# Weight loads in pieces between attention blocks, and routing steps moved among the expert tiles

## The chip, the cores and the metric

The kernel runs on one core of a Trainium2 chip. The metric is the device time of one execution in microseconds (us). The engines named below are TensorE (PE), VectorE (DVE), ScalarE (ACT), GpSimd (POOL) and SyncE (SP); SP, ACT and POOL also issue DMA transfers, which 16 DMA engines carry out.

## The reference

An attention over chunks, followed by a mixture of experts in which each token goes to one expert.

```python
for c in range(nc):                        # chunks of 32 queries
    q_c = q[:, :, c_start:c_end]
    k_full = concatenate([mem_k, k[:, :, l_start:r_end]])   # 8 memory rows, 16 left, 8 right
    a = softmax(scale * q_c @ k_full.T)
    out[:, :, c_start:c_end] = a @ v_full
x = out as (B, S, H * D)                   # 4 x 768 tokens of 512
logits = x @ w_gate                        # 8 experts
local_gate = sigmoid(x @ w_local)
for each b, s in order:
    e = argmax(logits) if s == 0 or local_gate < 0.5 else the expert of the token before
    out[b, s] = softmax(logits)[e] * (relu(x @ w1[e]) @ w2[e])     # 512 -> 1024 -> 512
```

All arrays are float32.

## The kernel before

**Attention.** The 4 x 768 queries of 8 heads are cut into 32 blocks of 96 queries (NB = 32, eight per batch). `load(n)` brings q and k of a block on SP's queue and v on ACT's. The tiles come from a pool of AHEAD + 1 buffers, and block n + AHEAD is loaded when block n begins. `scores` makes the transposed scores on TensorE (L215) and their exponentials on ACT (L220). `values` multiplies them by v (L227), and VectorE divides by the sums and writes the rows into the batch's tile x (L229, L230). There are three buffers for four x tiles (pool xp), so the tile of the fourth batch, opened at block 24, takes the buffer of the first. `turn(n)` transposes the rows of a block (L270), and after every fourth block `logits` makes the expert logits of four blocks (L277, L282).

**Routing.** It is done twice, each time for two batches. `route_picks` chooses experts on VectorE, and `route_ranks` counts, for each token, the earlier ones of its expert (transposes L329, scans L332 and L336). `route_places` turns ranks into places (L346, L350), and `route_rows` transposes them (L356) and has GpSimd scatter the rows of x into a DRAM table `x_dram` ordered by expert: 16 scatters of 96 rows of 2056 bytes (L372). `plan_early` lists the first five tiles of 128 rows (EARLY = 5), all of them of tokens from the first half. `plan_late`, after the second routing, lists the others, 26 at most.

**Experts.** A tile of 128 rows is gathered from `x_dram` by GpSimd (`gathered`, L484) into `xs`, one of five buffers. `rows_turned` transposes it on TensorE (L575), VectorE copies it to `gxt` (L577) and adds up `to`, the output rows (L579). `hidden` multiplies by w1 (L588) with the Relu on ACT (L590), `product` multiplies by w2 (L596), ACT scales the result (L598) and GpSimd scatters it to the output (L599). In the program's order the rows of tile i + 1 are turned between hidden and product of tile i. 24 tiles always run (SURE = 24), and up to seven more under a condition each; three of them ran here. `weights` loads an expert's w1 and w2, one transfer of 2 MB each (L499, L501), into one of three buffers, two tiles ahead; the first two experts' loads stand in the attention's loop, at blocks 22 and 26.

The order on each engine is set by a scheduler from the program's order and its model of when inputs are ready; each engine then works through its row of instructions strictly in order. On SP, q, k and weights share one queue. A DMA of SP or ACT also waits for the eighth one before it to have landed (eight semaphores in turn).

Of the kernel before, what the change touches and what calls it, by code (L numbers as in the profile page):

```python
# [8 lines left out]
F32 = mybir.dt.float32  # L9
# [33 lines left out]
AHEAD = 2  # L43
# [49 lines left out]
def everything(ctx, tc, q, k, v, w_gate, w_local, w1, w2, x_dram, out, ident, kept_i):  # L93
# [399 lines left out]

    def weights(tiles, i, pool):
        table, _, _ = tiles
        e = nc.values_load(table[:, i:i + 1], engines=[SP], min_val=0, max_val=E - 1,
                           skip_runtime_bounds_check_because="made from counts of tokens")
        w1_sb = pool.tile([P, DK, F], F32, name="w1_sb")
        nc.sync.dma_start(w1_sb, w1[bass.ds(e, 1)].rearrange("o p k f -> p (o k) f"))  # L499
        w2_sb = pool.tile([P, FK, D], F32, name="w2_sb")  # L500
        nc.sync.dma_start(w2_sb, w2[bass.ds(e, 1)].rearrange("o p m d -> p (o m) d"))  # L501
        return w1_sb, w2_sb
# [22 lines left out]
    for n in range(NB):  # L525
# [45 lines left out]
    def rows_turned(tiles, i, xs):  # L571
# [6 lines left out]
        to = hp.tile([P, 1], I32, name="to", bufs=4)  # L578
# [3 lines left out]
    def hidden(xt, w1_sb):  # L582
        ht = hp.tile([P, FK, P], F32, name="ht")
        for g in range(0, FK, 4):
# [5 lines left out]
            nc.scalar.activation(ht[:, g:g + 4], h_ps, ACT.Relu)  # L590
        return ht

    def product(ht, w2_sb, xs, to):
        y_ps = yps.tile([P, D], F32, name="y_ps")
        for m in range(FK):
# [3 lines left out]
        nc.gpsimd.indirect_dma_start(  # L599
            out=out, out_offset=bass.IndirectOffsetOnAxis(ap=to, axis=0), in_=y, in_offset=None,  # L600
            bounds_check=NT - 1, oob_is_err=False)
# [5 lines left out]
    for i in range(SURE):  # L607
        if i + 2 < EARLY:
            early_w.append(weights(early, i + 2, pools[(i + 2) % 3]))
        if i == 1:  # L610
            held["ranks"] = route_ranks()
        if i == 2:
            route_places(*held["ranks"])
            route_rows(1, (xs.pop(2), xs.pop(3)), *held["picks"], held["ranks"][1])
            late, n_i = plan_late(done)
        if i == 3 and not shifted:
            k_ps = xps.tile([1, 1], F32, name="k_ps", tag="xps")
            nc.tensor.matmul(k_ps, lhsT=kept, rhs=every, start=True, stop=True)
# [67 lines left out]
```

## Time and profile before

| what | value |
|---|---|
| median of 3 runs | 595.25 us (592.55 to 595.96) |
| profiled execution, its own time | 594.97 us |
| its span, from the first to the last instruction | 593.2 us |
| TensorE busy | 540.3 us, 91% of the span |
| mean granted TensorE clock | 0.941 of full speed |
| mean DMA rate over the span | 266 GB/s |

The span has two stages: attention until 160.33 us, where the first product of the experts begins, and the experts' tiles after it. In the page each digit of a row of slices stands for a fortieth of the span, 14.83 us; the row PEclk gives the granted clock in tenths. The chain of waits follows the work back from the last instruction, and each piece of it gives its start, its length and what it was.

### The profile page before, as it was taken

Reading aid. Unit: us, or ns where it says so; the run is one execution under the profiler, and the core shown is the slowest. Engines: PE = TensorE matmul, PEld = TensorE weight load, DVE = VectorE, ACT = ScalarE, POOL = GpSimd, SP = SyncE. Lnnn points to the kernel's source line nnn. Section 1 sums busy time; section 2 is a strip of 40 time slices with the busy share of each in tenths; the row PEclk is TensorE's granted clock in tenths of the full one; section 3 lists DMA queues with packets and bytes.
Section 4 is the critical chain, followed back from the end, with each engine's and each line's share of the span. In section 5 each row is a group of like instructions: output and inputs, shape, how many; then the busy total and the mean of one; then the engine's idle time right before and its main releaser. Section 6 shows DMA issues by size and latency. Waiting matters only on the chain.

```text
span 593.2 us, 8772 instructions
## 1 busy us (share of the span) xinstructions
PE 540.3 (91%) x3582; PEld 404.1 (68%) x3582; DVE 86.7 (15%) x319; ACT 112.1 (19%) x224; POOL 90.5 (15%) x112
## 2 busy tenths in 40 slices
PE   8999999495899990999999999999999999999980
PEld 6777778365677770877777777777777777766650
DVE  3333364111403400000000000000000000000000
ACT  3444444122111010011111111111111111111110
POOL 2000005330000642411111111111111100000000
PEclk9999999757799996799999999999999999999995
DMA  8666658996197998888888888889888888882000
GB/s 252 209 194 196 194 170 242 407 342 242 63 373 296 310 380 314 238 325 337 327 326 335 318 308 319 322 309 330 319 324 329 325 315 308 313 325 84 19 6 4
DMA packets 29427, 157.93 MB, mean 266 GB/s; under 512 B 5115, under 2 KB 9213, under 8 KB 22464
## 3 DMA queue, kind: packets, MB, share of 16 engines
q1 hardware_dynamic: 16992, 127.93, 59.2%
q0 software_dynamic: 6720, 20.78, 10.2%
q10 hardware_dynamic: 5664, 8.54, 5.0%
q8 instruction: 32, 0.52, 0.4%
q14 instruction: 19, 0.16, 0.1%
HBM read 144.62 MB, written 13.40 MB: 266 GB/s over the span
## 4 chain that ended last, share of the span: by engine, by line
PE 76%; DMA 10%; issue 8%; POOL 1%; DVE 1%; SPq 0%; ACT 0%; POOLq 0%; DVEq 0%
PE h_ps L588 28%; PE y_ps L596 25%; PE o_ps L227 8%; PE s_ps L215 6%; DMA x_dram<-x,row 4%; PE lt_ps L277 4%; DMA kt<-in_k_dram 3%; DMA out_dram<-y,to 2%; PE xt_ps L270 2%; PE g_ps L575 2%; POOL x_dram L372 1%; DMA xs<-x_dram,rows_late 1%; PE l_ps L282 0%; DVE rank L336 0%; PE c_ps L329 0%
## 5 line engine op out<-in xcount | busy, mean ns | idle before, releaser
L588 PEld LDWEIGHTS h_ps<-gxt,w_sb 128*128 128x128 f32 x1728 | 201.2, 196 | 28.4 <-DVE gxt L577 17.2
L588 PE MATMUL h_ps<-gxt,w_sb 128*128 128x128 f32 x1728 | 203.0, 279 | 17.6 <-DVE gxt L577 16.9
L596 PE MATMUL y_ps<-w_sb,ht 128*128 128x512 f32 x432 | 189.9, 592 | 0.0
L596 PEld LDWEIGHTS y_ps<-w_sb,ht 128*128 128x128 f32 x432 | 80.0, 190 | 90.4 <-issue 90.4
L599 POOL DMA_INDIRECT out_dram<-y,to x27 | 27.2, 1008 | 351.6 <-ACT y L598 334.3
L590 ACT ACTIVATE ht<-h_ps 128x512 f32<-128x512 f32 x54 | 32.2, 597 | 182.0 <-PE h_ps L588 182.0
L227 PE MATMUL o_ps<-vt,pt 128*96 128x65 f32 x512 | 58.1, 269 | 8.0 <-issue 7.8
L227 PEld LDWEIGHTS o_ps<-vt,pt 128*96 128x96 f32 x512 | 52.8, 182 | 11.2 <-issue 8.3
L215 PE MATMUL s_ps<-qt,kt 64*128 64x96 f32 x512 | 42.3, 297 | 5.6 <-DMA kt<-in_k_dram 5.6
L598 ACT ACTIVATE y<-y_ps,xs 128x512 f32<-128x512 f32 x24 | 16.5, 687 | 161.6 <-PE y_ps L596 161.6
L215 PEld LDWEIGHTS s_ps<-qt,kt 64*128 64x128 f32 x512 | 35.6, 200 | 14.3 <-issue 6.0
L372 POOL DMA_INDIRECT x_dram<-x,row x32 | 29.4, 918 | 102.9 <-DVE x L367 87.5
L579 DVE TENSOR_TENSOR to<-xs,past_late 128x1 int32<-128x1 f32 x19 | 3.0, 160 | 257.7 <-DMA out_dram<-y,to 229.9
L220 ACT ACTIVATE pt<-s_ps,mask_mid 128x256 f32<-128x256 f32 x72 | 29.0, 472 | 17.7 <-PE s_ps L215 17.4
L577 DVE COPY gxt<-g_ps 128x512 f32<-128x512 f32 x27 | 18.6, 690 | 83.8 <-PE g_ps L575 83.5
L230 DVE TENSOR_TENSOR x<-o_ps,rinvs 96x256 f32<-96x256 f32 x64 | 26.6, 417 | 13.0 <-DMA x_dram<-x,row 11.5
L277 PE MATMUL lt_ps<-xt,wg 128*9 128x384 f32 x64 | 23.7, 517 | 1.1 <-ACT xt L271 1.1
L229 DVE RECIPROCAL rinvs<-o_ps 96x4 f32<-96x4 f32 x64 | 11.3, 177 | 84.0 <-PE o_ps L227 82.9
L271 ACT COPY xt<-xt_ps 128x384 f32<-128x384 f32 x32 | 15.3, 479 | 39.9 <-PE xt_ps L270 39.9
L484 POOL DMA_INDIRECT xs<-x_dram,rows_late x19 | 18.4, 967 | 16.4 <-DMA x_dram<-x,row 10.9
L270 PE MATMUL xt_ps<-ident,x 96*128 96x96 f32 x128 | 18.0, 268 | 0.7 <-DVE x L230 0.7
L277 PEld LDWEIGHTS lt_ps<-xt,wg 128*9 128x9 f32 x64 | 5.4, 95 | 14.7 <-issue 12.5
(165 smaller groups left out, 141.8 us busy)
## 6 DMA issues: line engine op xcount, KB each, us to landing
w_sb<-in_w_dram SPq DMA_DIRECT2D x54, 2048.0 KB, 8.5
vt<-in_v_dram ACTq DMA_DIRECT2D x32, 260.0 KB, 3.7
kt<-in_k_dram SPq DMA_DIRECT2D x32, 256.0 KB, 3.7
qt<-in_q_dram SPq DMA_DIRECT2D x32, 192.0 KB, 3.3
x_dram<-x,row POOLq DMA_INDIRECT x32, 12.1
out_dram<-y,to POOLq DMA_INDIRECT x27, 7.5
xs<-x_dram,rows_late POOLq DMA_INDIRECT x19, 6.7
x<-x_dram,rows_late POOLq DMA_INDIRECT x7, 4.8
```

What stands on the lines that cost most here:

```text
L215: nc.tensor.matmul(st[:, u, a], lhsT=kt[h, a], rhs=qt[h, a], start=True, stop=True)
L220: nc.scalar.activation(pt[:, :, :, c], st[:, :, :, c], ACT.Exp, bias=m[:, g:g + 1], scale=SCALE)
L227: nc.tensor.matmul(o_ps[:, a], lhsT=pt[:, u, a], rhs=vt[:, 2 * a + u], start=True, stop=True)
L230: nc.vector.tensor_tensor(x[:, 0:D].rearrange("p (a u d) -> p u a d", u=2, d=DH)[:, u], o_ps[:, :, 0:DH], rinv.to_broadcast([QB, HP, DH]), ...
L270: nc.tensor.transpose(xt_ps[:, kk], x[:, P * kk:P * kk + P], identity=ident[:QB, :QB])
L277: nc.tensor.matmul(lt_ps, lhsT=wg[:, kk], rhs=xt[:, kk], start=(kk == 0), stop=(kk == DK - 1))
L372: ins = nc.gpsimd.indirect_dma_start(out=x_dram[:, :], out_offset=bass.IndirectOffsetOnAxis(ap=row[:, i:i + 1], axis=0), in_=x[b][0:QB, n] ...
L577: nc.vector.tensor_copy(xt, g_ps)
L588: nc.tensor.matmul(h_ps[:, m], lhsT=w1_sb[:, kk, P * (g + m):P * (g + m) + P], rhs=xt[:, kk], start=(kk == 0), stop=(kk == DK - 1))
L590: nc.scalar.activation(ht[:, g:g + 4], h_ps, ACT.Relu)
L596: nc.tensor.matmul(y_ps, lhsT=ht[:, m], rhs=w2_sb[:, m], start=(m == 0), stop=(m == FK - 1))
L599: nc.gpsimd.indirect_dma_start(out=out, out_offset=bass.IndirectOffsetOnAxis(ap=to, axis=0), in_=y, in_offset=None, bounds_check=NT - 1, o ...
```

## The change

The weights of an expert come in eight pieces of 0.5 MB: four of w1 (one for each 128 of its 512 rows) and four of w2 (each for two of its eight blocks of rows). Both arrays are laid out in DRAM so that a piece is one run of 512 KB, 4 KB to a partition; before, it was 16 KB to a partition. For the first two experts one piece is traced at each attention block from block 22 on, and what is left after the last block. AHEAD goes from 2 to 3. In the attention's loop `route_places`, `route_rows` and `plan_early` come one, one and two blocks earlier. Among the tiles, `route_ranks` moves from before tile 1's hidden to after tile 0's, `route_places` from tile 2 to before tile 1's hidden, and `route_rows` into the middle of that hidden. `to` gets eight buffers, the check sum `k_ps` moves by a tile, and the gathers for the conditional tiles are put behind the stores of the tiles before.

```diff
-AHEAD = 2
+AHEAD = 3
...
+    def weights_begun(tiles, i, pool):
...
+        def pieces():
+            e = nc.values_load(table[:, i:i + 1], engines=[SP], min_val=0, max_val=E - 1,
+                               skip_runtime_bounds_check_because="made from counts of tokens")
+            for k in range(DK):
+                nc.sync.dma_start(w1_sb[:, k], w1[bass.ds(e, 1), k].rearrange("o p f -> p (o f)"))
+                yield
+            for m in range(0, FK, 2):
+                nc.sync.dma_start(w2_sb[:, m:m + 2].rearrange("p m d -> p (m d)"),
+                                  w2[bass.ds(e, 1), m // 2].rearrange("o p d -> p (o d)"))
+                yield
...
-        nc.sync.dma_start(w1_sb, w1[bass.ds(e, 1)].rearrange("o p k f -> p (o k) f"))
-        nc.sync.dma_start(w2_sb, w2[bass.ds(e, 1)].rearrange("o p m d -> p (o m) d"))
...
+        if n == NR + 2:
+            route_places(*held["ranks"])
         if n == NR + 3:
-            route_places(*held["ranks"])
+            route_rows(0, (xs.pop(0), xs.pop(1)), *held["picks"], held["ranks"][1])
         if n == NR + 4:
-            route_rows(0, (xs.pop(0), xs.pop(1)), *held["picks"], held["ranks"][1])
+            early, done = plan_early()
         if n == NR + 6:
-            early, done = plan_early()
             early_xs = [gathered(early, i, (0,)) for i in range(EARLY)]
-            early_w = [weights(early, 0, wa)]
-        if n == NR + 10:
-            early_w.append(weights(early, 1, wa))
+            early_w, pieces = zip(*(weights_begun(early, i, wa) for i in range(2)))
+            early_w, pieces = list(early_w), itertools.chain(*pieces)
+        if n >= NR + 6:
+            next(pieces)
+    for _ in pieces:
+        pass
...
-        to = hp.tile([P, 1], I32, name="to", bufs=4)
+        to = hp.tile([P, 1], I32, name="to", bufs=8)
...
+            if between is not None and g == 0:
+                between()
...
+        between = None
         if i == 1:
-            held["ranks"] = route_ranks()
+            route_places(*held["ranks"])
+
+            def between():
+                route_rows(1, (xs.pop(2), xs.pop(3)), *held["picks"], held["ranks"][1])
         if i == 2:
-            route_places(*held["ranks"])
-            route_rows(1, (xs.pop(2), xs.pop(3)), *held["picks"], held["ranks"][1])
             late, n_i = plan_late(done)
...
-            gathered(late, SURE - EARLY + j, (0, 1), rest[:, j])
+            with tc.issue_after(stored):
+                gathered(late, SURE - EARLY + j, (0, 1), rest[:, j])
...
-        ht = hidden(xt, w1_sb)
+        ht = hidden(xt, w1_sb, between)
+        if i == 0:
+            held["ranks"] = route_ranks()
```

On SP, where the first expert's weights begin among the last loads of q and k, the kernel before has:

```order
L496 TENSOR_LOAD table_early_1268
L499 ISA
L499 DMA w1_sb_1305<-in_w1_dram 128x4096
L501 ISA
L501 DMA w2_sb_1307<-in_w2_dram 128x4096
L126 DMA qt_1402<-in_q_dram 128x384
L128 DMA kt_1404<-in_k_dram 128x512
L126 DMA qt_1441<-in_q_dram 128x384
L128 DMA kt_1443<-in_k_dram 128x512
L496 TENSOR_LOAD table_early_1268
L499 ISA
L499 DMA w1_sb_1483<-in_w1_dram 128x4096
```

At the same place the changed kernel has:

```order
L502 TENSOR_LOAD table_early_1196
L505 ISA
L505 DMA w1_sb_1308<-in_w1_dram 128x1024
L505 ISA
L505 DMA w1_sb_1308<-in_w1_dram 128x1024
L127 DMA qt_1358<-in_q_dram 128x384
L129 DMA kt_1360<-in_k_dram 128x512
L505 ISA
L505 DMA w1_sb_1308<-in_w1_dram 128x1024
L127 DMA qt_1411<-in_q_dram 128x384
L129 DMA kt_1413<-in_k_dram 128x512
L505 ISA
```

The two whole transfers ahead of four loads have become one or two quarter transfers between loads, and the second expert's weights, which stood ahead of the last two loads of q and k, come after all of them.

On TensorE, in the first three tiles (c_ps, b_ps and r_ps are the second routing's three steps), the kernel before has:

```order
L588 MATMUL h_ps<-gxt,w_sb 128x128 x32
L575 MATMUL g_ps<-ident,xs 128x128 x4
L596 MATMUL y_ps<-w_sb,ht 128x512 x8
L329 MATMUL c_ps<-ident,pick 48x96 x8
L588 MATMUL h_ps<-gxt,w_sb 128x128 x32
L575 MATMUL g_ps<-ident,xs 128x128 x4
L596 MATMUL y_ps<-w_sb,ht 128x512 x8
L346 MATMUL b_ps<-count_992,same 16x1
L346 MATMUL b_ps<-count_1835,earlier 16x1
L588 MATMUL h_ps<-gxt,w_sb 128x128 x6
L356 MATMUL r_ps<-ident,rank 96x16 x8
```

In the first two tiles the changed kernel has:

```order
L608 MATMUL h_ps<-gxt,w_sb 128x128 x32
L330 MATMUL c_ps<-ident,pick 48x96 x8
L595 MATMUL g_ps<-ident,xs 128x128 x4
L618 MATMUL y_ps<-w_sb,ht 128x512 x8
L347 MATMUL b_ps<-count_998,same 16x1
L347 MATMUL b_ps<-count_1823,earlier 16x1
L608 MATMUL h_ps<-gxt,w_sb 128x128 x16
L357 MATMUL r_ps<-ident,rank 96x16 x8
L608 MATMUL h_ps<-gxt,w_sb 128x128 x16
```

The counts stand ahead of tile 0's product, and the rows' transposes in the middle of tile 1's hidden instead of early in tile 2's.

On VectorE, from tile 3's copy on (`to` is the add for a late tile), the kernel before has:

```order
L577 COPY gxt_2037<-g_ps_2032 128x512
L619 CAST kept_i_66<-k_ps_2055 1x1
L579 TENSOR_TENSOR to_2180<-xs_1993,past_late_1971 128x1
L579 TENSOR_TENSOR to_2249<-xs_2058,past_late_1971 128x1
L577 COPY gxt_2109<-g_ps_2104 128x512
L579 TENSOR_TENSOR to_2318<-xs_2127,past_late_1971 128x1
```

From the same copy on the changed kernel has:

```order
L597 COPY gxt_2067<-g_ps_2062 128x512
L599 TENSOR_TENSOR to_2222<-xs_2023,past_late_2001 128x1
L599 TENSOR_TENSOR to_2297<-xs_2085,past_late_2001 128x1
L599 TENSOR_TENSOR to_2372<-xs_2160,past_late_2001 128x1
L597 COPY gxt_2142<-g_ps_2137 128x512
L599 TENSOR_TENSOR to_2447<-xs_2238,past_late_2001 128x1
L658 CAST kept_i_66<-k_ps_2212 1x1
L597 COPY gxt_2220<-g_ps_2215 128x512
```

Ahead of tile 4's copy stand the adds of tiles 5, 6 and 7, before those of 5 and 6; from there on the add of tile i + 3 is ahead of tile i's copy, before that of tile i + 2.

## Rows read from the trace of the kernel before

**Rows 1.** The page's slices: granted TensorE clock, tenths of full speed.
```profile
PEclk9999999757799996799999999999999999999995
```

**Rows 2.** Stretches: us, busy PE, PEld, DVE, ACT, POOL; PEclk, DMA share, GB/s.
```profile
10.00:90.00 80.00, 79.70 (x829) 63.78 (x828) 31.95 (x112) 38.75 (x93) 0.00 (x0) 1.00 0.65 196
...
105.00:134.00 29.00, 20.47 (x128) 15.61 (x127) 4.52 (x16) 6.22 (x15) 9.67 (x11) 0.65 1.01 373
...
196.00:223.00 27.00, 27.00 (x150) 18.78 (x148) 4.75 (x20) 3.08 (x5) 15.24 (x17) 1.00 0.99 349
...
300.00:400.00 100.00, 100.00 (x580) 73.21 (x580) 5.63 (x14) 12.83 (x21) 13.29 (x14) 1.00 0.86 325
```

**Rows 3.** The chain that ended last: start us, us, what; attention.
```profile
38.48 2.68 PE lt_ps L277 x8
...
49.62 1.06 PE s_ps L215 x16
50.68 1.50 PE o_ps L227 x16
...
53.58 2.68 PE lt_ps L277 x8
...
102.39 2.68 PE lt_ps L277 x8
...
105.47 7.77 issue
...
134.44 9.72 DMA kt<-in_k_dram
...
155.70 2.76 PE lt_ps L277 x8
...
160.33 9.01 PE h_ps L588 x64
```

**Rows 4.** VectorE in order of time: start us, us, instruction [idle before <-releaser].
```profile
112.72 0.75 DVE L230 TENSOR_TENSOR x<-o_ps,rinvs 96x256 f32<-96x256 f32 x2 [11.51 <-DMA x_dram<-x,row]
...
235.79 0.16 DVE L579 TENSOR_TENSOR to<-xs,past_late 128x1 int32<-128x1 f32 x1 [27.08 <-DMA xs<-x_dram,rows_late]
```

**Rows 5.** GpSimd in order of time, both rounds of scatters and two gathers.
```profile
92.21 0.98 POOL L372 DMA_INDIRECT x_dram<-x,row  x1 [87.47 <-DVE x L367]
...
112.91 0.91 POOL L372 DMA_INDIRECT x_dram<-x,row  x1 [1.62 <-DMA x_dram<-x,row]
...
195.50 0.91 POOL L372 DMA_INDIRECT x_dram<-x,row  x1 [1.44 <-DVE tiles_late L452]
...
216.40 0.91 POOL L372 DMA_INDIRECT x_dram<-x,row  x1 [0.62 <-DMA x_dram<-x,row]
...
231.73 0.98 POOL L484 DMA_INDIRECT xs<-x_dram,rows_late  x1 [10.90 <-DMA x_dram<-x,row]
...
315.23 0.97 POOL L484 DMA_INDIRECT xs<-x_dram,rows_late  x1 [0.30 <-issue]
```

**Rows 6.** Scatters into x_dram begun from 92 to 99 us: issue to landing.
```profile
DMA to landing us min/median/max: 4.4/6.8/8.5
```

**Rows 7.** Scatters into x_dram begun from 205 to 217 us: issue to landing.
```profile
DMA to landing us min/median/max: 11.7/14.7/17.3
```

**Rows 8.** SP's queue in order of time, the second expert's w2.
```profile
132.37 0.34 SPq L501 DMA_DIRECT2D w_sb<-in_w_dram  x1
```

**Rows 9.** TensorE in order of time: hidden of tile 4, and of two steady tiles.
```profile
237.50 10.26 PE L588 MATMUL h_ps<-gxt,w_sb 128*128 128x128 f32 x64 [14.33 <-DVE gxt L577]
...
312.70 7.31 PE L588 MATMUL h_ps<-gxt,w_sb 128*128 128x128 f32 x64
...
327.15 7.31 PE L588 MATMUL h_ps<-gxt,w_sb 128*128 128x128 f32 x64
```

**Rows 10.** Gathers (L484) from 300 to 400 us: issue to landing.
```profile
DMA to landing us min/median/max: 6.3/6.7/8.2
```

**Rows 11.** The page's DMA issues: queue, count, size, median us to landing.
```profile
kt<-in_k_dram SPq DMA_DIRECT2D x32, 256.0 KB, 3.7
```

More of the change, by code (lines that the diff above doesn't have):

```diff
@@ L1 @@
+import itertools
 from contextlib import ExitStack
@@ L492, in gathered @@
         return xs
-    def weights(tiles, i, pool):
[L495 to L498, printed above, removed]
-        nc.sync.dma_start(w1_sb, w1[bass.ds(e, 1)].rearrange("o p k f -> p (o k) f"))
-        w2_sb = pool.tile([P, FK, D], F32, name="w2_sb")
-        nc.sync.dma_start(w2_sb, w2[bass.ds(e, 1)].rearrange("o p m d -> p (o m) d"))
-        return w1_sb, w2_sb
+    def weights_begun(tiles, i, pool):
+        table, _, _ = tiles
+        w1_sb = pool.tile([P, DK, F], F32, name="w1_sb")
+        w2_sb = pool.tile([P, FK, D], F32, name="w2_sb")
+        def pieces():
[8 more added lines that the diff above has]
+                yield
+        return (w1_sb, w2_sb), pieces()
+    def weights(tiles, i, pool):
+        w, pieces = weights_begun(tiles, i, pool)
+        for _ in pieces:
+            pass
+        return w
     make_scores, make_values = (shifted_scores, shifted_values) if shifted else (scores, values)
@@ L577, in rows_turned, with hidden @@
         nc.vector.tensor_copy(xt, g_ps)
-        to = hp.tile([P, 1], I32, name="to", bufs=4)
+        to = hp.tile([P, 1], I32, name="to", bufs=8)
         nc.vector.tensor_tensor(to, xs[:, D + 1:XW], past[:, i:i + 1], op=ALU.add)
         return xt, to
-    def hidden(xt, w1_sb):
+    def hidden(xt, w1_sb, between=None):
         ht = hp.tile([P, FK, P], F32, name="ht")
@@ L609, in everything @@
             early_w.append(weights(early, i + 2, pools[(i + 2) % 3]))
+        between = None
         if i == 1:
-            held["ranks"] = route_ranks()
+            route_places(*held["ranks"])
+            def between():
+                route_rows(1, (xs.pop(2), xs.pop(3)), *held["picks"], held["ranks"][1])
         if i == 2:
-            route_places(*held["ranks"])
-            route_rows(1, (xs.pop(2), xs.pop(3)), *held["picks"], held["ranks"][1])
             late, n_i = plan_late(done)
-        if i == 3 and not shifted:
-            k_ps = xps.tile([1, 1], F32, name="k_ps", tag="xps")
-            nc.tensor.matmul(k_ps, lhsT=kept, rhs=every, start=True, stop=True)
-            nc.vector.tensor_copy(kept_i, k_ps)
         if late is not None:
@@ L628, in everything @@
             j = i + 8 - SURE
-            gathered(late, SURE - EARLY + j, (0, 1), rest[:, j])
+            with tc.issue_after(stored):
+                gathered(late, SURE - EARLY + j, (0, 1), rest[:, j])
         w1_sb, w2_sb = early_w[i]
-        ht = hidden(xt, w1_sb)
+        ht = hidden(xt, w1_sb, between)
+        if i == 0:
+            held["ranks"] = route_ranks()
+        if i == 4 and not shifted:
+            k_ps = xps.tile([1, 1], F32, name="k_ps", tag="xps")
+            nc.tensor.matmul(k_ps, lhsT=kept, rhs=every, start=True, stop=True)
+            nc.vector.tensor_copy(kept_i, k_ps)
         if i + 1 < SURE:
@@ L634, in everything @@
             ahead = rows_turned(tiles, at_i, early_xs[i + 1])
-        product(ht, w2_sb, early_xs[i], to)
+        stored = product(ht, w2_sb, early_xs[i], to)
         xt, to = ahead
```

10 lines of the change are left out of this document (6 added, 4 removed).

## The prediction

> **What bounds the kernel now.** I read the page's slices first. TensorE is busy in nearly all of them, but its granted clock is below full in slices 8 to 11 and in 16 and 17 [rows 1]. The table by stretches gives the places: from 105 to 134 us a mean of 0.65 between its two levels (1.2 and 2.4 GHz), against 1.00 before 90 and after 300 [rows 2]. So three stalls and the half-speed stretches behind them are what can be won. The rest is TensorE's own work: a group of four attention blocks takes 15.10 us (53.58 minus 38.48 [rows 3]) and a tile of the expert stage 14.45 us (327.15 minus 312.70 [rows 9]).
>
> Stall 1 is the 7.77 us of "issue" at 105.47 [rows 3]. The profile names no releaser for it, but VectorE does: it sat 11.51 us until 112.72, when it could write x of block 24 [rows 4]. That block opens the fourth batch's x tile, whose buffer is the first batch's; the write waits for that batch's eight scatters. They went out from 92.21 on [rows 5], and the pair of 2 MB weight loads was queued among them. Scatters begun before 99 us landed in 6.8 us (median) [rows 6].
>
> Stall 2 is the 9.72 us that a k load took from 134.44 [rows 3]. Its issue stood on SP behind a 2 MB weight load which left only at 132.37 [rows 8], and its bytes stood behind that load in the queue.
>
> Stall 3 is the 14.33 us until 237.50 [rows 9]. Tile 4's rows were long there; VectorE's copy of them stood behind an add for tile 5 that waited 27.08 us for a gather [rows 4]. That gather left at 231.73, after the last of 16 scatters, begun at 216.40 [rows 5]. Those scatters took 14.7 us to land [rows 7], with the DMA engines busy for 0.99 of the time [rows 2].
>
> **The change part by part.** *Attention's end (stalls 1 and 2).* TensorE's sequence now has the transposes that give the scatters their rows ahead of the fifth logits product (2.68 us [rows 3]) and some of the values around it: the scatters begin about 4 us earlier, near 88. The eighth begins 7 x 1.38 = 9.7 us later (15 steps from 92.21 to 112.91 are 1.38 each [rows 5]) and lands 6.8 us after that [rows 6], so x is free at 104.5. The values of block 25 come at 105.47 [rows 3] and need VectorE's writes of block 24 before (0.75 [rows 4]): the stall is 0 to 1 instead of 7.77. Beside these scatters stand now two pieces of 0.5 MB instead of 4 MB. In SP's order every q and k load comes before the second expert's weights, with one or two pieces between loads, and AHEAD = 3 issues each load a block (2.9 us) earlier; at most three pieces (1.6 MB, 4.3 us at the 373 GB/s of [rows 2]) are in front of one. So stall 2 goes; its bounds are 0 and that 4.3 less the block won.
>
> What the stage then costs: two more groups after the sixth logits product at 102.39 put the eighth at 132.6, and hidden(0) follows 160.33 - 155.70 = 4.63 later [rows 3], at 137.2. That is too long by what the last group lacks: between the sixth and the eighth product the new order has one set of values fewer (1.50) and three sets of scores fewer (1.06 each), and about 1 us of transposes and a copy's wait more: 133.5 is the floor. I take 135.0: the work is counted, and 1.5 us is left for the two waits above. So hidden(0) starts **25.3 us earlier** (23.1 to 26.8).
>
> *Clock behind them.* hidden(0) took 9.01 us against 7.31 at full speed [rows 3, 9]: **1.7 us** back, if no stall is left before it.
>
> *Second routing (stall 3).* The rows' transposes stand after 16 of tile 1's 32 products in the new order, before after 6 of tile 2's: one tile less 10/32 of a hidden of 7.31, 12.2 us earlier. Before, the first scatter began at 195.50 [rows 5], 35.2 us after hidden(0); now 35.2 - 1.7 - 12.2 = 21.3 after it. Fifteen steps of 1.39 (195.50 to 216.40 [rows 5]) put the last at 42.2. What it takes to land is not shown for 4 KB weight rows: 6.8 us beside the attention's loads, whose rows are 1.5 to 2 KB [rows 6], and 14.7 beside weight rows of 16 KB [rows 7]. I take 9, since 4 KB is nearer to the first: 51.2. Then gathers 5 and 6, the store of tile 2 and gather 7 leave at about 1 us each (0.98 [rows 5]), gather 7 lands 6.7 later [rows 10], and the add and copy take 0.9: 61.8. The new order on VectorE has three adds (tiles 5, 6, 7) ahead of tile 4's copy, before it had two, so the whole chain counts. TensorE wants that copy at 237.50 - 14.33 - 160.33 - 1.7 = 61.1. The stall is 1 us (0 to 6.4) instead of 14.33: **13.3 us** saved, and the 10.26 us of the next hidden go back to 7.31 [rows 9]: **3.0 us**, if the stall is that short.
>
> The Trainium skill, "DMA: Bandwidth & Descriptors", section "Queues, rings and completion order", says each DMA engine goes round its queues and changes only after a whole packet. By that rule a 2 KB scatter row gets a third of a full engine beside 4 KB rows and a ninth beside 16 KB rows; 3.2 MB of scatters at a third of 373 GB/s would take 25 us, and the stall would be near 0. That agrees in kind with the 6.8 and 14.7 us of [rows 6, 7].
>
> *Steady tiles.* Weight bytes are the same, in rows of 4 KB instead of 16. At 16 KB rows the engines moved 325 GB/s at a share of 0.86, so 378 when full; at the attention's rows 196 at 0.65, so 301 [rows 2]. Drawn as a line in time per row (100 ns at 1.9 KB, 693 at 16 KB), 4 KB gives 190 ns, some 345 GB/s. A tile moves 325 x 14.45 = 4.70 MB: 13.6 us, under the 14.45 of TensorE. I take 0; the share should rise to about 0.94. The cover is thin: at 301 it is 15.6. Eight issues a tile on SP instead of two, at 0.34 us each [rows 8], are 2.7 us of 14.45. Eight target buffers for the add take away its wait for old stores, which nothing on TensorE waited for. But the add for tile i+3 now leads the copy for tile i: gather i+3 leaves 315.23 - 312.70 = 2.5 us after product i-2 ends, lands 6.7 later, and 0.9 follow: 10.1 of the 14.45 us. Hidden, with 4.3 us to spare (8.2 is the longest landing [rows 10]).
>
> *Start.* A third load of 0.71 MB before block 0: 0 if it queues behind, 2.4 us at 301 GB/s if it shares; I take 0.3.
>
> **Sum**, against the profiled execution (594.97, span 593.2, so 1.8 outside it; the median of the runs, 595.25, is 0.3 above): 593.2 - 25.3 - 1.7 - 13.3 - 3.0 + 0.3 = 550.2, and with 1.8 **552 us**.
>
> **The rivals.**
> *A. Scatters are as slow as before.* If landing stays at 14.7 us, stall 3 keeps about 6.4 us and its half-speed stretch: 552 + 5.4 + 3 = 560. For it: the engines were full there [rows 2] and as many bytes remain. Against: smaller rows, an earlier start.
> *B. Attention keeps a wait.* More is moved before hidden(0) in less time. One wait of 4 us with the half-speed stretch that followed stall 1 (0.65 over 29 us [rows 2] is 20 us at the lower level, 10 lost) gives 552 + 14 = 566.
> *C. The DMA engines become the bound.* At 301 GB/s a tile takes 15.6: 22 tiles x 1.15 = 25 us, 577. Against: the line above.
> *D. Slower: the gather enters the tile's loop.* With the add for tile i+3 ahead of copy i, every microsecond of landing above 11.0 (6.7 + 4.3) lengthens each of 16 tiles (5 to 20). At 14.7 us, seen with full engines [rows 7], it is 16 x 3.7 = 59: 611. It undoes the gain from 13.7 us on. Against: 8.2 is the longest landing in steady tiles [rows 10].
> *E. Nothing comes of it:* the weights' arrival, not these waits, sets the end; 595. Against: the steady tiles follow each other at 14.45 us with no gap [rows 9], so weights come in time.
> *F. Pieces land one after another.* A 256 KB load takes 3.7 us to land [rows 11]; eight pieces in series, at that price at least, are 30 us a tile: 25 tiles x 15 = 375, so 925. Against: the attention's three loads per 2.9 us block land in 3.7 each and overlap. The Trainium skill, "DMA: Bandwidth & Descriptors", section "Measured (HBM→SBUF, 128 partitions, SWDGE, issued from GpSimd)", asks for batches of 1 MiB or more and a fit of 2.0 us plus bytes at 436 GB/s; by that, 0.5 MiB is 3.2 us and eight in series 26. It holds for one transfer at a time.
>
> **How the numbers follow.** Forecast 0.58, A 0.14, B 0.12, C 0.08, D 0.04, E 0.03, F 0.01. The forecast's own bounds are 23.1 to 26.8, a stall of 0 to 6.4 and a start of 0 to 2.4; all at their best is 549. The range 548 to 569 holds forecast, A and B (0.84). Over 0.5% faster (about what a measurement of this kernel tells from no change): 0.92; within 0.5%: 0.03; slower: 0.05.
>
> **What would show it.** Right: no gap near 105, hidden(0) at 135 (133 to 138), the granted clock at 1.00 until then; second scatters from 21 us after it, the stall before tile 4's hidden at 0 to 3 us; tiles of 14.45 at a DMA share of 0.90 to 0.96. Wrong: k loads waiting for pieces; scatters landing in over 12 us; VectorE's add released by a gather after TensorE is idle in tiles 5 to 20.

## The result, and the profile after

| kernel | median | runs | ratio to before |
|---|---|---|---|
| before | 593.9 us (589.88 to 595.96) | 4 | |
| changed | 560.9 us (560.47 to 561.71) | 4 | 0.9454 (95% interval 0.9398 to 0.9509) |

552 us was predicted, in a range of 548 to 569. The profiled execution took 560.47, with a span of 558.7. All later runs, below, were on chips 3, 10 and 1, and there the same two kernels are only 14 us apart. The chip of the first measurement is not recorded, so that it was another one is not shown, though the expectations speak of a first and a second chip. What follows up to the experiments is the first measurement.

The page's slices of the changed kernel, granted TensorE clock and DMA share in tenths:

```profile
PEclk9999997998999999999999999999999999999995
DMA  8766655999699999899998988888999998880000
```

The table by stretches (columns as in [rows 2]):

```profile
10.00:90.00 80.00, 78.93 (x825) 64.72 (x822) 32.88 (x116) 38.46 (x92) 0.03 (x1) 0.98 0.66 200
...
105.00:134.00 29.00, 25.94 (x228) 18.40 (x230) 7.69 (x27) 9.76 (x25) 8.07 (x9) 0.88 1.04 385
196.00:223.00 27.00, 27.00 (x152) 19.03 (x152) 1.89 (x7) 3.17 (x5) 5.87 (x6) 1.00 0.98 380
300.00:400.00 100.00, 100.00 (x580) 73.22 (x579) 5.42 (x14) 13.17 (x21) 15.71 (x16) 1.00 0.88 323
```

From 105 to 134 us the clock is 0.88 instead of 0.65, and TensorE is busy for 25.94 of 29 us instead of 20.47. The chain of waits shows which stalls are left. It has the third one no more: hidden of tile 4 (206.07) follows the product of tile 3 at once, where 14.33 us lay in [rows 9]. Of the second one something is left: a k load that left SP only when a weight piece sent at 102.75 had landed, and a logits product (126.21) at half speed behind it:

```profile
102.75 14.38 DMA w_sb<-in_w_dram
117.15 7.76 DMA kt<-in_k_dram
...
126.21 4.89 PE lt_ps L278 x8
...
145.00 7.38 PE h_ps L608 x64
...
206.07 7.23 PE h_ps L608 x64
```

TensorE and VectorE in order of time, at stall 1 and stall 2. The x buffer is waited for 2.04 us instead of 11.51 [rows 4], and costs TensorE 0.92:

```profile
104.35 0.17 DVE L370 COPY x<-token 96x8 f32<-96x8 f32 x1 [2.04 <-DMA x_dram<-x,row]
...
105.10 1.54 PE L228 MATMUL o_ps<-vt,pt 128*96 128x65 f32 x16 [0.92 <-DVE rinvs L230]
...
125.04 1.17 PE L216 MATMUL s_ps<-qt,kt 64*128 64x96 f32 x8 [2.96 <-DMA kt<-in_k_dram]
```

GpSimd in order of time: the second round's first and last scatter, and the first gather that needs them all; below it the issue to landing of those 16 scatters:

```profile
166.31 0.94 POOL L373 DMA_INDIRECT x_dram<-x,row  x1 [3.64 <-DVE x L368]
...
184.81 0.91 POOL L373 DMA_INDIRECT x_dram<-x,row  x1 [0.31 <-issue]
...
194.66 0.99 POOL L485 DMA_INDIRECT xs<-x_dram,rows_late  x1 [7.64 <-DMA x_dram<-x,row]
```

```profile
DMA to landing us min/median/max: 5.2/7.8/9.7
```

### The profile page after: what moved, and what is told of

Same layout as the page of the kernel before. It is cut to its first block, busy times and chain, and to the rows that moved or that the text cites. A ratio compares the mean times of both kernels' runs of the same rounds, so it can differ in the third digit from the quotient of the medians.

```text
span 558.7 us, 9286 instructions
## 1 busy us (share of the span) xinstructions
PE 530.2 (95%) x3582; PEld 391.9 (70%) x3582; DVE 87.1 (16%) x319; ACT 111.8 (20%) x224; POOL 90.8 (16%) x112
## 4 chain that ended last, share of the span: by engine, by line
PE 83%; DMA 7%; issue 6%; DVE 1%; ACT 0%; SPq 0%; POOL 0%; POOLq 0%; DVEq 0%; ACTq 0%
PE h_ps L608 31%; PE y_ps L618 30%; PE o_ps L228 7%; PE s_ps L216 5%; PE lt_ps L278 4%; DMA out_dram<-y,to 3%; DMA w_sb<-in_w_dram 3%; PE g_ps L595 2%; PE xt_ps L271 2%; DMA kt<-in_k_dram 1%; PE z_ps L123 1%; PE l_ps L283 0%; DVE rank L337 0%; PE c_ps L330 0%; PE r_ps L357 0%
## 5 line engine op out<-in xcount | busy, mean ns | idle before, releaser
L608 PEld LDWEIGHTS h_ps<-gxt,w_sb 128*128 128x128 f32 x1728 | 196.8, 192 | 14.4 <-issue 9.6
L608 PE MATMUL h_ps<-gxt,w_sb 128*128 128x128 f32 x1728 | 198.5, 275 | 3.3 <-DVE gxt L597 2.5
L228 PE MATMUL o_ps<-vt,pt 128*96 128x65 f32 x512 | 52.6, 252 | 1.3 <-DVE rinvs L230 0.9
L228 PEld LDWEIGHTS o_ps<-vt,pt 128*96 128x96 f32 x512 | 47.1, 165 | 5.2 <-issue 1.9
L216 PE MATMUL s_ps<-qt,kt 64*128 64x96 f32 x512 | 40.9, 289 | 3.0 <-DMA kt<-in_k_dram 3.0
L216 PEld LDWEIGHTS s_ps<-qt,kt 64*128 64x128 f32 x512 | 34.1, 192 | 11.9 <-issue 7.7
L278 PE MATMUL lt_ps<-xt,wg 128*9 128x384 f32 x64 | 25.4, 546 | 0.6 <-ACT xt L272 0.6
L272 ACT COPY xt<-xt_ps 128x384 f32<-128x384 f32 x32 | 15.3, 478 | 26.1 <-PE xt_ps L271 22.9
L271 PE MATMUL xt_ps<-ident,x 96*128 96x96 f32 x128 | 16.5, 252 | 0.3 <-DVE x L231 0.3
L278 PEld LDWEIGHTS lt_ps<-xt,wg 128*9 128x9 f32 x64 | 5.6, 98 | 15.3 <-issue 13.9
```

The lines of the kernel that those rows point to most:

```text
L216: nc.tensor.matmul(st[:, u, a], lhsT=kt[h, a], rhs=qt[h, a], start=True, stop=True)
L228: nc.tensor.matmul(o_ps[:, a], lhsT=pt[:, u, a], rhs=vt[:, 2 * a + u], start=True, stop=True)
L271: nc.tensor.transpose(xt_ps[:, kk], x[:, P * kk:P * kk + P], identity=ident[:QB, :QB])
L278: nc.tensor.matmul(lt_ps, lhsT=wg[:, kk], rhs=xt[:, kk], start=(kk == 0), stop=(kk == DK - 1))
L608: nc.tensor.matmul(h_ps[:, m], lhsT=w1_sb[:, kk, P * (g + m):P * (g + m) + P], rhs=xt[:, kk], start=(kk == 0), stop=(kk == DK - 1))
```

## The experiments

There are twelve runs: c_before to e6 on chip 3, k1 to k3 on chip 10, e8 on chip 1. Two of them are the changed kernel and the kernel before themselves. Each ratio is to runs of the kernel before taken beside the run (medians of 601.1 to 602.6 us), so runs on different chips are compared by their ratios. hidden(0) is the start of the first expert product; the last column is the time from there to hidden of tile 4, in which the second routing lies.

| run | median, us | ratio to before (95%) | hidden(0) | to hidden(4) |
|---|---|---|---|---|
| c_before | 602.01 (one run) | | 170.59 | 74.7 |
| c_after | 587.05 | 0.9755 (0.9735 to 0.9774) | 159.78 | 75.0 |
| e1_whole16 | 597.68 | 0.9919 (0.9886 to 0.9952) | 170.30 | 73.1 |
| e2_whole | 597.63 | 0.9923 (0.9876 to 0.9970) | 168.03 | 74.3 |
| e3_after_loads | 588.74 | 0.9778 (0.9733 to 0.9823) | 160.25 | 74.6 |
| e4_old_blocks | 583.51 | 0.9690 (0.9659 to 0.9720) | 154.30 | 73.5 |
| e5_ahead2 | 588.30 | 0.9798 (0.9768 to 0.9828) | 158.88 | 74.0 |
| e6_old_tiles | 588.27 | 0.9783 (0.9765 to 0.9801) | 159.77 | 73.7 |
| k1_two_bursts | 588.22 | 0.9780 (0.9722 to 0.9837) | 159.02 | 72.3 |
| k2_burst_alone | 602.53 | 1.0009 (0.9967 to 1.0052) | 170.57 | 73.9 |
| k3_old_two_bursts | 586.92 | 0.9737 (0.9698 to 0.9776) | 156.64 | 74.1 |
| e8_pieces_alone | 582.34 | 0.9709 (0.9654 to 0.9764) | 154.16 | 73.4 |

In the first measurement these two columns were 160.33 and 77.2 before, 145.00 and 60.9 after.

**Pieces and row size.** Both runs put back two transfers of 2 MB per expert at blocks 22 and 26; they have one order of instructions on all engines and differ in the rows alone, 16 KB or 4 KB.

```diff
-            for k in range(DK):
-                nc.sync.dma_start(w1_sb[:, k], w1[bass.ds(e, 1), k].rearrange("o p f -> p (o f)"))
+            nc.sync.dma_start(w1_sb, w1[bass.ds(e, 1)].rearrange("o p k f -> p (o k) f"))   # e1: 16 KB
+            nc.sync.dma_start(w1_sb, w1[bass.ds(e, 1)].rearrange("o k p f -> p (o k) f"))   # e2: 4 KB; w2 likewise
...
+            early_w = [weights(early, 0, wa)]
+        if n == NR + 10:
+            early_w.append(weights(early, 1, wa))
```

> The changed kernel with weights loaded as before the change: two transfers of 2 MB per expert, rows of 16 KB, the first two experts at blocks 22 and 26; all routing steps stay where the change put them, and AHEAD stays 3. It has the same instruction order as the next run, and differs from it in the row size alone. Row-size theory (the prediction's): the second round's scatters land in about 14.7 us as in the kernel before, the copy of tile 4 waits about 6 us, so hidden of tile 4 starts 67 us after hidden of tile 0 instead of 61.1; with the k loads behind 2 MB transfers again hidden(0) is at 150 to 158 instead of 145: 572 to 585 in all. Rival (scatters land faster because they start earlier or meet less traffic, not because of the rows): they land in 8 to 9 us as in the changed kernel, no wait at tile 4, 566 to 575, and the same time as the next run.

> The changed kernel with two transfers of 2 MB per expert at blocks 22 and 26, but rows of 4 KB: the same as the run before except for the rows. Row-size theory: scatters of the second round land in 8 to 9 us, hidden(4) starts 61 us after hidden(0), and the run is 6 to 9 us shorter than with 16 KB rows. Rival: no difference from 16 KB rows. Against the changed kernel it shows what the pieces and their places are worth: if pacing is what removed the wait for k, hidden(0) is at 150 to 158 and the total 566 to 575; if the row size did it, hidden(0) is at 145 and the total 561.

Measured: 597.68 and 597.63. The row size makes no difference to the time in these runs. That does not settle the first measurement, for in both runs VectorE waits for TensorE while the second round's scatters go out (10.80 us in e1, 13.54 in e2, of the new kind described below), and such a wait covers what slower scatters would cost. The landing of each scatter is not in these traces, but GpSimd's rows in e1 show the last scatter and the first gather that needs them all:

```profile
213.37 0.91 POOL L373 DMA_INDIRECT x_dram<-x,row  x1 [0.97 <-issue]
...
221.05 0.98 POOL L485 DMA_INDIRECT xs<-x_dram,rows_late  x1 [3.89 <-DMA x_dram<-x,row]
```

With weight rows of 16 KB all had landed 7.7 us after the last one left; in the kernel before it was 15.3 (216.40 to 231.73 [rows 5]). So 16 KB rows alone do not make the long landing. There was less traffic beside it, though (205 GB/s from 214 to 221 us in e1, 389 from 216 to 231 in the kernel before), so what the rows are worth beside full engines stays open.

Both runs are 10.6 us slower than the changed kernel there (587.05), of which hidden(0) has 8.2 (e2) and 10.5 (e1). Waits for k are back, 1.49 us in e2 and 2.35 in e1, where c_after has none. So in the later runs the 10.6 us come from the size and the places of the transfers, not from the rows. The rest of the change still leaves both runs some 5 us below the kernel before (0.992, both intervals below 1).

**Pieces behind all k loads.**

```diff
-        if n >= NR + 6:
-            next(pieces)
-    for _ in pieces:
-        pass
+    with tc.issue_after(k_loads[-1]):
+        for _ in pieces:
+            pass
```

> The changed kernel with every weight piece of the first two experts put behind the last load of k on SP; nothing else moves on any engine. Theory (the k wait of 2.96 us at 125 us and the half-speed stretch behind it come from pieces ahead of the last q and k loads on SP): no wait at 125, granted clock 1.00 from 115 to 134, hidden(0) at 139 instead of 145, total 555. Rival 1 (the DMA engines are full with scatters and gathers anyway, so k is late whoever is ahead): hidden(0) stays at 144 to 146, 561. Rival 2 (the first expert's weights become the last thing to arrive): 8 pieces begun at about 117 land by 130 at 380 GB/s, so no wait at hidden(0); if they start only at 125, it waits until 138 to 140 for w1 and its product for w2: 556 to 560.

Measured: 588.74 and hidden(0) at 160.25, as in c_after. But c_after has no wait for k in the later runs, since another wait comes first, so this doesn't decide whether it would save the 2.96 us of the first measurement. That stays open. It does show that in the later runs the places between the blocks bring nothing: pieces behind all k loads do as well. Transfers of 2 MB behind all k loads were not run, so the size and the place of the transfers are not told apart.

**The changed kernel and the kernel before, once more.** The four runs so far had waits of a new kind, and their kernel before took 602.6 us.

> The changed kernel itself once more, as the measure for the runs beside it. In the four runs so far VectorE, ScalarE and TensorE's weight loads sat 10 to 19 us in waits put down to something remote, each while GpSimd sends its scatters; neither kernel's first trace has such a wait, and the kernel before took 602.6 beside them instead of 593.9. Theory 1 (it comes with the chip): here, if it is the same chip, the changed kernel has such waits too and takes 575 to 590; on a chip like the first it has none and takes 561. Theory 2 (it comes from the order of instructions in those four kernels): the changed kernel takes 561 wherever it runs.

> The kernel before, for its trace beside the changed one's on the same chip. Theory 1 (the remote waits come with the chip): waits of 10 us and more put down to something remote while GpSimd scatters, on top of the three stalls, and 600 to 604 us. Theory 2 (they come from the order of instructions): none, and 593 to 596.

Measured: 587.05, and 602.01 for the kernel before (one run; seven beside c_after have a median of 601.09), both with such waits. Theory 2 falls, since the first traces of the same two kernels have none. Theory 1 fits, as three chips have such waits in every later run; but what else differed between the first measurement and the later ones is not known, so that it is the chip is not shown. The chain of waits of c_after has one of them as its longest piece ahead of the expert tiles (first fence); the second fence is its table by stretches:

```profile
95.16 16.13 another core or an unknown queue
```

```profile
92.00:99.00 7.00, 3.87 (x38) 3.31 (x37) 1.39 (x8) 0.00 (x0) 5.17 (x7) 0.76 0.71 200
99.00:105.00 6.00, 0.00 (x0) 0.00 (x0) 0.00 (x0) 0.00 (x0) 4.48 (x6) 0.50 0.53 162
105.00:110.00 5.00, 0.00 (x0) 0.00 (x0) 0.00 (x0) 1.21 (x3) 2.28 (x3) 0.50 0.74 236
```

From 99 to 105 us TensorE, VectorE and ScalarE do nothing at all (columns two to five), while GpSimd sends its scatters; the clock falls to its lower level. I call this a hold-up. VectorE's and ScalarE's waits, and the first and last scatter of that round, in order of time on each engine:

```profile
111.27 0.18 DVE L441 COPY sums_early<-s_ps_early 128x17 f32<-128x17 f32 x1 [16.11 <-remote]
...
105.00 1.21 ACT L221 ACTIVATE pt<-s_ps,mask_last 128x256 f32<-128x256 f32 x3 [13.33 <-remote]
...
88.67 0.98 POOL L373 DMA_INDIRECT x_dram<-x,row  x1 [83.93 <-DVE x L368]
...
106.98 0.91 POOL L373 DMA_INDIRECT x_dram<-x,row  x1 [0.30 <-issue]
```

Both waited for products of TensorE, the scores of L216 and the sums of L434. TensorE's rows have these long before:

```profile
92.80 1.14 PE L216 MATMUL s_ps<-qt,kt 64*128 64x96 f32 x16
...
95.52 0.45 PE L434 MATMUL s_ps_early<-ident,total 8*128 8x8 f32 x2
```

They end at 93.94 and 95.97, 11 and 15 us before ScalarE and VectorE go on; in the first measurement both went on within 0.2 us, the copy after a wait of 0.76. (The ends of matmuls are modelled, so whether the product or its signal was late is not shown.) c_before has the same (VectorE 7.70 us until 106.54, ScalarE 12.39 until 110.10). Of the 33 us gained at first, stall 3's part is missing in the later runs: to hidden(4) both kernels take 75 us.

**Scatters alone.** Sixteen scatters more, into a table that nobody reads, from block 9 in program order; the scheduler began them as soon as their rows were ready, in groups of two and four.

```diff
+        if n == 9 and not shifted:
+            for i in range(16):
+                ins = nc.gpsimd.indirect_dma_start(
+                    out=spare[:, :], out_offset=bass.IndirectOffsetOnAxis(ap=spare_row[:, i:i + 1], axis=0),
+                    in_=xs[0][0:QB, i % NQB, 0:D], in_offset=None).ins
```

> The changed kernel with 16 more scatters, of 96 rows of 2 KB each, from the first batch's x into a spare table that nobody reads, at block 9 of the attention, where GpSimd otherwise has nothing to do for 50 us and no weights are on the way. Nothing on TensorE, VectorE or ScalarE moves or waits for them in the program. Theory (a run of scatters by itself holds up the other engines on the second chip): near 40 to 60 us VectorE and ScalarE sit 8 to 16 us in waits put down to something remote, TensorE idles behind them, its clock falls, and the total is 10 to 20 us above the changed kernel's 587. Rival (it takes the routing's own instructions, or weights on the queues, as well): no such wait before 88 us, and the total within 2 us of 587. On a chip like the first: no wait and 561 to 563.

Measured: 602.53, 15.5 above the changed kernel (ratios 1.0009 and 0.9755). The last four of these scatters, and ScalarE and VectorE in order of time:

```profile
42.74 0.91 POOL L561 DMA_INDIRECT spare<-x,spare_row  x1 [1.66 <-DVE x L231]
43.96 0.91 POOL L561 DMA_INDIRECT spare<-x,spare_row  x1 [0.30 <-issue]
45.18 0.92 POOL L561 DMA_INDIRECT spare<-x,spare_row  x1 [0.30 <-issue]
46.40 0.91 POOL L561 DMA_INDIRECT spare<-x,spare_row  x1 [0.30 <-issue]
...
48.58 0.47 ACT L221 ACTIVATE pt<-s_ps,mask_mid 128x256 f32<-128x256 f32 x1 [3.24 <-remote]
...
48.61 0.18 DVE L230 RECIPROCAL rinvs<-o_ps 96x4 f32<-96x4 f32 x1 [3.91 <-remote]
```

Both engines go on together, 1.3 us after the last scatter's end. The first four, from 13.69 on, do the same: VectorE waits 4.15 us until 19.54, ScalarE 3.27 until 19.50, and TensorE then runs at 0.50 from 24 to 32 us. The second logits product is at 50.21 instead of 39.54. The pairs in between bring no such wait of over 1.5 us. So a run of GpSimd's scatters holds up the other engines in these runs without routing or weights; whether by its issue or by its traffic is not told apart. The waits are shorter than expected; a good part of the price is the half-speed stretch behind them.

**Two bursts of eight.** With the change's blocks, and with those of before:

```diff
         for b in range(PAIR):
+            if b == 1:
+                yield
...
+        if n == NR + 7:      # NR + 8 with the old blocks
+            with tc.issue_after(writes[-1]):
+                next(held["rows"], None)
+            early_xs = [gathered(early, i, (0,)) for i in range(EARLY)]
```

> The changed kernel with the first round's 16 scatters in two bursts of eight: the second batch's two columns of x are written by VectorE only at block 23, so its eight scatters, and the five gathers behind them, start about 104 instead of following at once; TensorE's order is the same. On the second chip the changed kernel's 16 scatters ran from 88.7 to 107.9 and VectorE sat 16.1 us, until 111.3, in one wait for TensorE put down to something remote; ScalarE sat 13.3. Theory (the waits are tied to a run of GpSimd's scatters: they set in some 6 us after its start and end some 4 us after its last issue): the first wait ends at 101 to 103, a second of 5 to 8 us follows behind the second burst, hidden(0) at 150 to 156 instead of 159.8, total 578 to 584 on that chip. Rival 1 (they come from something else at that place of the program): the wait still ends at 111, hidden(0) at 160, total 587. Rival 2 (any eight scatters cost what sixteen do): two waits of 13 us, hidden(0) at 165 or later, total 592 or more. On a chip like the first: no such waits, 559 to 563.

> The attention's routing steps at their blocks of before (as in the run that did this alone, 583.5 on the second chip) and the first round's scatters in two bursts of eight, the second at block 24. Theory (waits tied to runs of scatters; the late places save 3 to 5 us there): both gains add, hidden(0) at 146 to 152 against 154.3 with the old blocks alone, total 574 to 580, the shortest of these kernels on that chip. Rival (two bursts do nothing, or cost): 583 or more. On a chip like the first it keeps a wait for the x buffer near 107 of 2 to 5 us that the changed kernel has not: 560 to 566.

Measured: 588.22 and 586.92, no gain. In k1 the first wait did end early, at 99.03, 2 us after the eighth scatter's end, so it is tied to the burst, as the theory had it. But the second burst (108.16 to 117.6) and the five gathers behind it brought waits of their own, of 5.06 (ScalarE) and 5.44 us (VectorE, until 129.77), and hidden(0) is at 159.02, not 150 to 156. No forecast fits whole: the waits are shorter than rival 2 had them, and the total is rival 1's.

**The parts undone.** e4 puts back the attention's routing steps, e6 the tiles', e8 both, so that pieces and AHEAD = 3 are left; e5 puts back AHEAD.

```diff
-        if n == NR + 2:                     # e4, e8: + 3, + 4 and + 6 again
-            route_places(*held["ranks"])
...
-            def between():                  # e6, e8: in tile 2 again, ranks before tile 1
-                route_rows(1, (xs.pop(2), xs.pop(3)), *held["picks"], held["ranks"][1])
...
-AHEAD = 3                                   # e5 alone
+AHEAD = 2
```

> The changed kernel with the attention's routing steps back at their blocks of before (places one block later, rows one, the early plan two); the expert tiles' routing stays. Theory (the half-speed stretch at 85 to 97 us comes from the places' product standing on TensorE ahead of the counts it needs): the fifth logits product takes 2.7 us again instead of 3.9 and starts 3 to 3.5 us earlier, at 87.2; the scatters begin 3 to 4 us later in relation to it, so block 24's write of x waits longer and the gap near 105 grows from 0.9 to 3 to 6 us, with a half-speed stretch behind it: 561 to 570. Rival (the dip has another cause, such as the work VectorE has there): the fifth product still takes 3.9 us, and only the loss near 105 is added: 565 to 574.

> The changed kernel with AHEAD = 2. Theory (the third load before block 0 costs the 1.5 us by which the first logits product came later, 24.9 instead of 23.4): it starts at 23.4 again, and the loads of q and k are issued a block later, so the wait for k near 125 grows from 3 to about 5 us: total within 2 us of the changed kernel beside it. Rival (the third load is what keeps k in time): the wait for k grows to 6 us and more with a longer half-speed stretch, 5 us or more slower than the changed kernel.

> The changed kernel with the second routing's steps back at their places among the tiles (ranks before tile 1's hidden, places and rows in tile 2); weights in pieces and the attention's order stay. Theory (the earlier place is worth 12.2 us of lead, and the scatters' faster landing some 6): the first scatter 33 to 35 us after hidden(0) instead of 21.3, the last at 54, landed at 62, gathers 5 to 7 and VectorE's add until 73; tile 4's copy, wanted at 61.1, is 12 us late or, if only gather 5 counts, 4 to 6, and the half-speed stretch behind costs 3: 8 to 15 us slower than the changed kernel. Rival (landing of the scatters set stall 3, not the place): no gap at tile 4, the same time as the changed kernel.

> The changed kernel with all routing steps back at their places of before, in the attention and among the tiles: what is left of the change is the weights in pieces and AHEAD = 3. On the later chips, with 601 to 602 for the kernel before, putting back the attention's steps gave 583.5 and the tiles' steps 588.3, against 587.05 for the whole change. Theory (where scatters hold up the other engines, the moved steps save nothing, since the hold-up takes the place of the waits that they remove, and the pieces are the whole gain): hidden(0) at 153 to 156, hidden(4) 72 to 76 us after it, total 582 to 588. Rival (each move alone is covered by the other, both together are not): the 14 us wait before tile 4 is back on top of the hold-up, hidden(4) 80 us or more after hidden(0), total 592 or more. On a chip like the first, theory and rival agree: the wait before tile 4 is back, about 16 us slower than the changed kernel, 572 to 580.

Measured: e4 583.51, e5 588.30, e6 588.27, e8 582.34, against 587.05.

The attention's steps at their earlier blocks cost 3.5 us in the later runs (the intervals of e4 and c_after don't meet): with the old blocks hidden(0) is at 154.3 instead of 159.8. The fifth logits product is at 85.59 and 88.42; 1.15 us of that is the start, 1.7 the moved work ahead of it, which the stretch behind it has no more. What is left is the hold-up: up to the sixth product TensorE idles 13.5 us in e4 and 15.6 in c_after. e4's own question, whether the moved work brings the half-speed stretch, could not be answered, for c_after has none there either (the product takes 2.75 us in both); nor can the expected gap near 105 be seen, because the hold-up covers it.

e5 is level with c_after (the intervals overlap), with no wait for k. e6 is level: the tiles' early steps gain nothing there, and the hold-up stands where stall 3 was (VectorE waits 16.81 us in one piece until 217.51), so it does not size them for the first measurement. In e8 3.27 us of a wait for the copy come back, before tile 3, and it is still no slower than the whole change. So in the later runs the pieces, with what else e8 keeps (AHEAD = 3, eight buffers for `to`, the later gathers), bring the whole gain by themselves. The parts do not add up: without the pieces the moved steps are worth some 5 us (e1, e2), beside them nothing. e4 and e8 are the shortest kernels there; neither ran beside the first measurement.

## Why the prediction was right or wrong

**Total.** 550.2 was the predicted span, 558.7 came. In the sum hidden(0) is due at 135.3 (135.0 and 0.3 for the start); it came 9.7 us later. hidden(4) then followed after 60.9 us instead of the sum's 62.2, and the tiles behind it took 0.1 us longer. The range holds the result because it was made wide enough for rival B, and a loss of B's kind came. It is luck, too, that it holds: in the later runs the same kernel takes 587 us, above the range, by a hold-up that no rival names.

**Stall 1** (0 to 1 us): 0.92. Right, by misses that cancel: the scatters began at 89.97, not 88, but the eighth came 8.6 us behind the first (9.7 reckoned) and landed in 5.8 (6.8), and the x buffer was written at 104.35 (104.5 predicted).

**hidden(0) at 135.0** was the term that was mis-sized: 145.00. The ten us lie in three stretches: 1.6 up to the first logits product, 4.1 from the fourth to the sixth, 4.4 from there to hidden(0).

First, the start: 0.3 was reckoned, the first logits product came 1.55 later than before (24.86 against 23.30). The third load isn't shown to be the cause: c_before has 24.85, e4 with three loads 23.29, e5 with two 23.67. A start read from one execution is uncertain by 1.5 us.

Second, from the fourth product to the sixth it is 37.8 us instead of 33.7. The moved steps are hardly any of it. Ahead of the fifth product they cost 1.7 us (18.7 in c_after, 17.0 in e4), which the step named but didn't price, and behind it the same work is missing. What is left is 0.92 of stall 1 and 3.0 of clock: 1.9 ahead of the fifth product and 1.2 in it (3.91 instead of 2.75).

Third, stall 2: from the sixth logits product to hidden(0) 37.0 us instead of the 32.6 reckoned.

The clock ahead of the fifth product, from the rows of TensorE and the table by stretches, first of the changed kernel and then of c_after:

```profile
84.00:92.00 8.00, 7.34 (x49) 5.39 (x49) 3.95 (x15) 2.46 (x6) 1.72 (x2) 0.64 0.46 137
...
84.91 0.18 PE L347 MATMUL b_ps<-count,earlier 16*16 16x1 f32 x2 [0.66 <-DVE rinvs L230]
...
90.70 3.91 PE L278 MATMUL lt_ps<-xt,wg 128*9 128x384 f32 x8
```

```profile
84.00:92.00 8.00, 7.50 (x62) 5.01 (x62) 3.82 (x16) 2.62 (x6) 2.72 (x3) 1.00 0.61 189
...
84.50 0.18 PE L347 MATMUL b_ps<-count,earlier 16*16 16x1 f32 x2 [0.66 <-DVE rinvs L230]
...
88.42 2.75 PE L278 MATMUL lt_ps<-xt,wg 128*9 128x384 f32 x8
```

The same gap of 0.66 us is followed by half speed in one execution (0.64 granted from 84 to 92 us) and not in the other (1.00). Of the nine runs with this order here, three have it (this one, e2 and e3: the product takes 3.91 or 5.28 us) and six do not (2.75). The sign "1.00 until 135" thus failed at a place where the prediction saw no stall, and it can fail or hold by chance.

**Stall 2** ("goes; its bounds are 0 and 4.3 less the block won"): 2.96 us, outside these bounds (4.3 less a block of 2.9 is 1.4), and the next logits product took 4.89 instead of 2.75. This is rival B in small. The step looked at the order on SP alone, at most three pieces ahead of a load. SP's queue shows what it missed, the time at which the load leaves:

```profile
110.85 0.34 SPq L505 DMA_DIRECT2D w_sb<-in_w_dram  x1
111.38 0.34 SPq L508 DMA_DIRECT2D w_sb<-in_w_dram  x1
115.66 0.34 SPq L127 DMA_DIRECT2D qt<-in_q_dram  x1
117.15 0.34 SPq L129 DMA_DIRECT2D kt<-in_k_dram  x1
```

SP issued nothing between 111.7 and 115.66. SP's waits in the trace name the reason: the q load stood 3.9 us until an earlier k load, sent at 101.71, had landed, and the k load behind it 1.1 us until the weight piece of 102.75 had (the 14.38 us in the chain above). That is the waiting for an older transfer's semaphore, which the step left out. Then k landed 7.76 us after its issue, where the engines moved 385 GB/s at a share of 1.04; the median k load of before took 3.7 [rows 11]. A load behind pieces pays for the landing of older transfers as well as for the bytes ahead of it.

**Stall 3.** Right, step by step: scatters from 21.3 us after hidden(0) (21.3 predicted), the last at 39.8 (42.2; they came every 1.23 us, not 1.39), landed after 9.85 (9), the copy's chain done at 60.8 (61.8), hidden(4) at 60.9 with no stall, and with 0.1 us to spare. The clock behind the stalls came back as reckoned (hidden(0) 7.38 us, hidden(4) 7.23; 7.31 reckoned). The reason given for the landing is weaker than the number. The Trainium skill, "DMA: Bandwidth & Descriptors", section "Queues, rings and completion order", has each DMA engine go round its queues packet by packet. The first measurement agrees in kind with what the prediction makes of that, that smaller weight rows let scatters through (the last nine scatters landed in a median of 8.4 us beside 4 KB rows, 14.7 beside 16 KB rows [rows 7]). But start and traffic changed with the rows; e1 and e2, where the rows alone differ, take the same time; and in e1 the scatters are down in 7.7 us beside 16 KB rows. In the later runs the whole term of 13.3 and 3.0 us is absent, and no row of the kernel before's trace could have told that.

**Steady tiles.** Right: 14.45 us, no gap. The share was 0.88 to 0.91, not 0.94: 323 GB/s at 0.88 are 367 with the engines full, where the line drawn through two row sizes gave 345. Gathers landed in 7.9 us (median, 300 to 400 us) instead of 6.7 [rows 10], so the slack that rival D spoke of went from 4.3 to 3.1 us.

**Rivals.** The time came out near the sums of A and B (560, 566), but of these only B's mechanism is in the trace; that the time is A's is chance, for A's landing was short. C: share 0.91 at most. D: no add was released by a gather behind an idle TensorE. E: refuted, faster in the first measurement and in c_after. F: pieces overlap; 0.5 MB each moved 323 to 385 GB/s, level with 2 MB transfers (325 to 373 [rows 2]). (Its sum is 927, not 925.) The Trainium skill, "DMA: Bandwidth & Descriptors", section "Measured (HBM→SBUF, 128 partitions, SWDGE, issued from GpSimd)", asks for 1 MiB; with several on the way no run here shows a loss by half of that. The fit that the prediction names beside it stands in that page's section "Anatomy of one DMA — SWDGE (gpsimd) path".

## What to carry to other kernels

Keep a long weight load from standing ahead of small loads in the same queue. Pieces did that in every measurement here, whether placed between the small loads or behind them; whole transfers behind them were not tried. The last small load behind pieces must still be priced with the landing of what is ahead of it. Moving a step earlier pays only where it removes a wait that nothing else would fill. Measure more than once, and on more than one chip, before reading a gain off one trace: a stall that was removed may be covered by another that this trace doesn't have.

## What the runs showed of the hardware

**Indirect DMAs of GpSimd in a row can hold up the other engines.** In the later runs, on chips 3, 10 and 1, not in the first measurement: from 4 scatters (3 to 4 us) to 16 (up to 18.9, ScalarE in k2_burst_alone's routing), ending 1 to 6 us after the last one or within the burst. The waits fall on instructions that wait for another engine: VectorE and ScalarE for TensorE, weight loads for VectorE. The Trainium skill, "SBUF — State Buffer", section "Who interferes with whom", knows one contention between engines, the port that GpSimd and VectorE share. Here ScalarE's 13.33 us and VectorE's 16.11 in c_after are both waits for TensorE, whose rows end 11 and 15 us earlier, so that port alone doesn't explain it. The later traces also lack records: c_after has 5651 of the 6480 signals by which its DMAs tell of their landing, the first trace of the changed kernel all 6480, and most of the missing ones fall into the two rounds of scatters. Whether the recording is held up by the same thing or has a part in it is not shown. What holds the engines up, and why the first measurement had none, is open.

**Half speed behind short gaps is not fixed.** The same order of instructions had the stretch behind a gap of 0.66 us in three runs and not in six.
